# Query maxima that join the output products as exp(2m) in ten of sixteen head groups, in a fused linear-attention and MLP kernel

## The chip, the cores and the metric

The kernel runs on one core of a Trainium2 chip. Such a core has a matrix engine (TensorE, PE in the profile, with its weight loads as PEld), a vector engine (VectorE, DVE), an activation engine (ScalarE, ACT), a general engine (GpSimd, POOL) and a queue engine (SyncE, SP), which work side by side and wait for one another through semaphores. The metric is the device time of one execution in microseconds, lower is better. Matrix products land in PSUM, which has eight banks; everything else lies in SBUF.

## The reference, cut to what matters

```python
# q, k, v: (8 batches, 8 heads, 576 positions, 64); w_phi: (64, 128), all float32
def phi(x):
    proj = np.einsum('bhsd,df->bhsf', x, w_phi)
    proj = proj - np.max(np.abs(proj), axis=-1, keepdims=True)      # m, one per position
    return np.concatenate([np.exp(proj), np.exp(-proj)], axis=-1)
q_p, k_p = phi(q), phi(k)
kv  = np.einsum('bhsf,bhsd->bhfd', k_p, v)
z   = np.sum(k_p, axis=2)
num = np.einsum('bhsf,bhfd->bhsd', q_p, kv)
den = np.einsum('bhsf,bhf->bhs', q_p, z)[..., None] + 1e-06
x   = (num / den)        # -> rows of (batch, position), columns of (head, 64): 4608 x 512
h   = x @ w_in                                                       # 512 -> 2048
g   = np.where(h > 0.0, h, np.exp(np.minimum(h, 0.0)) - 1.0)         # ELU
out = g @ w_out                                                      # 2048 -> 512
```

The maximum m is taken of the absolute value and is subtracted before the sign: one half of the features is exp(p - m), the other exp(-(p - m)) = exp(-p + m). The maximum therefore does not cancel in num / den: the two halves carry the factors exp(-m) and exp(m), and their ratio is exp(2m).

## The kernel before

The 64 pairs of batch and head are worked on in 16 groups of four heads, two groups per batch. Heads lie in pairs: a 64-deep product uses one half of the rows of the array, and two products with different halves ("par" 0 and 1) stand side by side. The kernel is written as small steps, each with a letter, and a long string (`ORDER`) fixes the order in which the steps are issued; every engine works through its own instructions in that order. A digit behind a letter is the PSUM bank.

For each group, the maxima of |q w_phi| are found by a projection with positions on the partitions (`m_mm`, `m_max`). They are then needed with features on the partitions. So each maximum is split into two bf16 numbers (`m_split`), transposed on TensorE (`m_pe`), copied (`m_copy`), and subtracted from the projection by a matmul with a selector matrix of zeros and minus ones (`sel`), which accumulates on the projection:

```python
def m_split(n, part):
    ...
        mq = st["mq", n][:, :, p[0]:p[1]]
        eng = nc.gpsimd if n < PE_TRANSPOSED else nc.vector      # PE_TRANSPOSED = 4
    eng.tensor_copy(hi, mq)                                      # cast fp32 -> bf16   (L328)
    eng.tensor_tensor(mhl[n % 2][:, :, NI + p[0]:NI + p[1]], mq, hi, op=ALU.subtract)  # (L329)

def m_pe(n, part, bank=None):
    tr = transposes(bank)
    nc.tensor.transpose(tr[:, 0, :], mhl[n % 2].rearrange("p r x -> p (r x)"), ident)  # (L335)

def m_copy(n, part):
    nc.vector.tensor_copy(st["mT", n], st["trm", n][:, 0:1, :])                        # (L340)

def q_mm(n, c, bank=None):
    ...
            nc.tensor.matmul(                                    # the projection (L371)
                places(par, j, m), w_sb[rows, :], qT[rows, i:i + m, :]..., start=(x == 0), stop=False)
    for j in range(w):
        for par in range(2):
            nc.tensor.matmul(                                    # minus the maximum (L381)
                places(par, j, 1), sel[rows, p0 + j, :], mT[rows, 0, :],
                start=False, stop=(j == w - 1))

def q_exp(n, c, sg):                                             # ScalarE, both signs (L393)
    nc.scalar.activation(Eq[:, sg, ...], st["pq", n, c]..., ACT.Exp, scale=1.0 - 2.0 * sg)
```

The output products add the two halves of the features in PSUM, and VectorE divides:

```python
def x_mm(n, part, bank=None):
    for hi in range(2):
        for x, (pr, t) in enumerate(parts):
            for sg in range(2):                                  # (L439)
                nc.tensor.matmul(pn[:, hi, x, :], Eq[:, sg, hi, par, i0 * D:(i0 + 2) * D],
                                 kv_sb[:, hi, pr, sg, :], start=(sg == 0), stop=(sg == 1))

def x_div(n, part):
    nc.vector.tensor_scalar_add(den, pn[:, :, :, D], 1e-6)       # (L453)
    nc.vector.reciprocal(rec, den)                               # (L454)
    nc.vector.tensor_tensor(xp..., pn[:, :, :, 0:D], rec..., op=ALU.mult)              # (L456)
```

Other steps that the text speaks of: the k projection (`k_mm`, L238), the q projection for the maxima (`m_mm`, L294), the scaling of v by the exp of the k maxima on GpSimd (`v_scale`, L275), the products of keys and values (`kv_mm`, L409; copied out of PSUM by VectorE in L419), the DMA transposes of q and k (L227) and of the attention output (`x_dma`). The MLP works in nine chunks of 512 rows: `h_mm` (L510), exp on ScalarE (`h_exp`, L521), a clamp on GpSimd in place (`h_min`, `e_sb`, L526), a last step on VectorE (`h_elu`, L530), then `o_mm` (L538), a copy out of PSUM on ScalarE (`o_copy`, L548) and the store. The transposed attention output is held whole in SBUF (`xT_sb`, 512 x 4608); a chunk is 512 neighbouring columns of it, which belong to two batches in most chunks.

Of the kernel before, what the change touches and what calls it, by code (L numbers as in the profile page):

```python
# [10 lines left out]
FP32 = mybir.dt.float32  # L11
# [7 lines left out]
eabefegcj7dfkA0gj7BfkBeA2CA4hBl7gl6Bmj1mj0hBCM6iBkkA2DCBFEl1NDA4Bl0EmBOCFP1BEA6QBmS2CEM0CTU4eNDB  # L19
EUTOEM6VM0DP3NW4EQNM6S2NM0OTFENU6TXP1FOUQS2VP5Y4Tj1ZS6QTl0W4mTS2kTj0XTW6TkS4XA0Tj3BY2ZA6Tkl2Bp3m  # L20
Y5BCqBZrA0p4sCM2qp5rNM6qDrBNp3l2sqp7BmrsqM4rp6NFp2qsqrp5srp4CqOqrP7l3srW0sgQmp6sEj7XqS2DTrEkM0p5
NY7qTsrS0sFp4EZTsM2M6TNp5EqNS0qrp3Trp2sOsTA6fp4CqU0qrrUBssVqA2Bp5rW0sBP7p6Xqnt4qrBrsp1QCp5zqp7qr
sp0qrszW2DsrqFsS5rEp1sTXp7qp0Trfsp3qA1rtBesqp7ECoqp6qtDrBrsp5rzsqEp0sqS1qztTrrsFTsp7EU5uS1qrUrTs
A3Vt0TCtsBW1oW5BXp7A3qtCzrtsBXzt7BnM1A5M3NBtuCztDFNEM0BztNgM2uvt6ODENP7M0nM4QNES2tTNFTfS0S4TEA2t
CTp7TTU0UBA4VtBCp1qorBW2sqp0vBOXrp7quP5p4rzQsDqFW2sqrzp6XrA0qEp5szBsp3rqCvp7rqseBp4vsrqp6DsrqS0s
rM2Tp5NFEqp7sqrp3qrsTp4rsqsM0qA5rt2CEp7NBrtsBsM0qS5NtrTEsTS0U3oTA5UCTtVBt7OnBP4W0QuS3XvW5TtDXzTE
tztfFA0EuzS2M4Bt6NTztCTS4BM2otDTEtzTFA0Eut7CntNgBA4BM2CtNtBBA0OU2CUDuP6p5VQM2qM6Np4rNEp3qBsW6rqp
2sBrp5XqFeW0qsrzS6DXrp4TEzTp3sqEsvM0S6Np2TFnEqS0Tp5rqrsU6qzrUsTrp4TzOsp3qVorA0qsA6p2Brsvsp5qCP4r
p3qQCBrp4qsW0qrst2DXBEp5BFsW0zrqtEszXS6rtTvsM0A3NtBnTt5CztDBFEM0S6zNM3TtENTU0guA3S6UTotVBvt2BtTC
p1OA3qW6urp0XBP5tBQztqCzS5uA3t7DCTEntsDBFtrBEsW1TtXEA3uM5ep0NzBEp7Cqvp6rBFsM1qp5NqrM3qrS0Np2Trsf  # L30
p4qsTp7rqOsp6qrsP5rS0qQsU2oTrUsTS4Vvp7TsW0TzS2qXA4p6rBgTzp1Cqt0svqrTp7rszDW2sBEp6Xqp5rqzstrqsrA1
S3M6EsTotCFtNDt5BEtBETM6U1NFA3UBM6VtuNBvW0tCnXA6M2Bt4NBtCW0tODXuEp7vP6EA0QM2BtzNfqp6Cuzrp5BzS2qM
0Dt4rNTzFtETssvS0EU2TS6qtFoOTrtTesUTA0nVp5uCW2zqP7p6BXrvgp4BQsqzS2qA0rp7CTrzp5sqBsrp6Dsp4BEqM0qp
7NrTrsW0qsqA2rp5BXEp6BsFqp1rCqrp4sDrqsS2rp7sTEsqA5t0BrTtCFEqU1sBrUA3sS5BtVoTCtTzA1Bt7CuzW3DBEtXn
BtEDM0M2zFNW4EtXFt6nEuNM0U4vOM2NUP7tNtQVS0M2S4TNp7TOtTt3TqS0A4rop2BTtCvTtszqA0BrtCzup7sDBzp6qW4r
qvp2uXEBp3rqszA0qM4rsp7FNzrp6qECvp5sBrp4sqsp2qrDrqP7p3Qsqrp7BsrsqS5qA0srp4Brst2EqsBp3FTECp7qtrTr
sqtsrM0U4sUNA6tBVM0BS3Nt5CtODtTFEW0uP7TtEQXS2uA6t4TzCtBzW0BtXDTFtEzW0uEp7XzS2U4TzUTS0Vvt6qTrS2vT
p5Tzp4TW0qp3XqrtrqszW0rp7Xzp2qszp1rsqtsrqzsp5rsvp7sp4p3tp2uqp1vqrqt6rsqp0rsqrsqtrsqp7rsrsp5qsp4r
qsp3rqstrqsp7rstqp5rsp4qp7rqst3rqsp5rstqtrstp7t5qp4rsp2qtrqsp7rsp4qtrqsp2rstqp7rsp4qut2ruvsqp6rv
tqsutrvstt7ttp6p5qtrqsp4rst6qtrsp5tqp4rsp3qp5rqsp1rqsutrqvsut4ruvsttvtt7p6p5qtrqsup3rvstqp6rstp5  # L40
uqp4vqrp7qrsp3rsqst6rqstrsttt7utvttt6utvttt7utvttuv
# [4 lines left out]
def kernel(  # L46
# [34 lines left out]

    consts = ctx.enter_context(tc.tile_pool(name="consts", bufs=1))
# [5 lines left out]
    moep = ctx.enter_context(tc.tile_pool(name="moep", bufs=2))  # L88
    epool = ctx.enter_context(tc.tile_pool(name="epool", bufs=4))
# [24 lines left out]
    xT_sb = consts.tile([P, N_CT, NTOK], BF16)  # L114
    FULL = 4 * P

    def full_col(b):
        return (b // 2) * 2 * S + (b % 2) * (FULL + P)

    def mixed_col(b):  # L120
        return (b // 2) * 2 * S + FULL + (b % 2) * D

    def out_rows(tile_index):
        bp, t = divmod(tile_index, 9)
        rows = []
        for half in range(2):
            if t == 4:
                b, s = 2 * bp + half, 8
            else:
                b, t4 = (2 * bp, t) if t < 4 else (2 * bp + 1, t - 5)  # L130
                s = 4 * (t4 // 2) + t4 % 2 + 2 * half
            rows.append(
                out[b * S:(b + 1) * S, :].rearrange("(p s) c -> s p c", s=NS)[s]
            )
        return rows
# [11 lines left out]
    PIECES = (((0, 4), (4, 7), (7, 9)), ((0, 3), (3, 6), (6, 9)))  # L147
    TILES = (
# [56 lines left out]


# [12 lines left out]
    def t_copy(name, n, j0, j1):  # L219
        nc.vector.tensor_copy(  # L220
            get((name + "T", n), new_t(name))[:, j0:j1, :],
            st["tr", name, n, j0][:, 0:j1 - j0, :],
        )

    def t_dma(name, n):
        nat = st[name, n // 2][:, 2 * (n % 2):2 * (n % 2) + 2]
        nc.sync.dma_start_transpose(  # L227
            out=get((name + "T", n), new_t(name)),
            in_=nat.rearrange("p r s d -> p (r s d)"),
        )  # L230
# [56 lines left out]
    def m_mm(n, c, bank=None):  # L287
        own = min(n // FIRST, 1)
        p0, p1 = PIECES[own][c]
        pj = two_banks(bank).rearrange("p r (i f) -> p r i f", f=F)  # L290
        for j in range(p1 - p0):
            for par in range(2):
                rows = slice(par * D, (par + 1) * D)
                nc.tensor.matmul(  # L294
                    pj[:, par, j, :],
                    st["qT", n][rows, PLACE_OF[own][par][p0 + j], :],
                    w_sb[rows, :],
                    start=True,
                    stop=True,
                )  # L300
        st["pm", n, c] = pj

    def m_max(n, c):
        p0, p1 = PIECES[min(n // FIRST, 1)][c]
        if n < FIRST and c == 0:

            mq = st["pm", n, c][:, 0, 0, 0:2 * p1].rearrange("p (r i) -> p r i", r=2)
            st["mq0", n] = mq
        else:
            mq = get(("mq", n), lambda: small.tile([P, 2, NI], FP32, name="mq"))  # L310
            mq = mq[:, :, p0:p1]
        nc.vector.tensor_reduce(  # L312
            mq, st["pm", n, c][:, :, 0:p1 - p0, :], axis=AX.X, op=ALU.max,
            apply_absolute_value=True,
        )

    def m_split(n, part):
        if n < FIRST:
            p = ((0, 4), (4, NI))[part]
        else:  # L320
            p = (0, NI)
        hi = mhl[n % 2][:, :, p[0]:p[1]]
        if n < FIRST and part == 0:
            mq, eng = st["mq0", n], nc.vector
        else:
            mq = st["mq", n][:, :, p[0]:p[1]]
            eng = nc.gpsimd if n < PE_TRANSPOSED else nc.vector
        eng.tensor_copy(hi, mq)  # L328
        eng.tensor_tensor(  # L329
            mhl[n % 2][:, :, NI + p[0]:NI + p[1]], mq, hi, op=ALU.subtract  # L330
        )
# [6 lines left out]
    def m_copy(n, part):  # L338
        st["mT", n] = tpool.tile([P, 1, P], BF16, name="mT")
        nc.vector.tensor_copy(st["mT", n], st["trm", n][:, 0:1, :])  # L340


    def q_mm(n, c, bank=None):
# [3 lines left out]
        qT, mT = st["qT", n], st["mT", n]  # L347
# [17 lines left out]
        for x in range(max(len(r) for r in runs)):  # L365
            for par in range(2):
                if x >= len(runs[par]):
                    continue
                j, i, m = runs[par][x]
                rows = slice(par * D, (par + 1) * D)  # L370
                nc.tensor.matmul(  # L371
                    places(par, j, m),
                    w_sb[rows, :],
                    qT[rows, i:i + m, :].rearrange("p i (h t) -> p h i t", h=2),
                    start=(x == 0),
                    stop=False,
                )
        for j in range(w):
            for par in range(2):
# [4 lines left out]
                    mT[rows, 0, :],  # L384
# [32 lines left out]
    def kv_copy(n):  # L417
        st["kv", n] = work.tile([P, 2, 2, 2, D + 1], BF16, name="kv_sb")
        nc.vector.tensor_copy(  # L419
# [10 lines left out]
    def x_mm(n, part, bank=None):  # L430
        Eq, kv_sb = st["Eq", n], st["kv", n]
        parts = x_parts(n, part)
# [30 lines left out]

    def x_pe(n, part, bank=None):
# [8 lines left out]
    def x_copy(n, part):  # L473
# [3 lines left out]
        c0 = full_col(b) + part * 2 * P  # L477
        nc.vector.tensor_copy(
            xT_sb[:, 2 * g:2 * g + 2, c0:c0 + 2 * P].rearrange(
# [4 lines left out]
        if part == 1:  # L484
            nc.vector.tensor_copy(
                xT_sb[:, 2 * g:2 * g + 2, mixed_col(b):mixed_col(b) + D],
# [3 lines left out]
    def x_dma(n, pr, mixed):  # L490
        b, g = divmod(n, 2)
        xp, ct = st["xp", n, pr], 2 * g + pr
        if not mixed:
            nc.sync.dma_start_transpose(
                out=xT_sb[:, ct, full_col(b):full_col(b) + FULL].rearrange(
# [4 lines left out]
        else:  # L500
            nc.sync.dma_start_transpose(
                out=xT_sb[:, ct, mixed_col(b):mixed_col(b) + D].unsqueeze(1),
# [4 lines left out]
    def h_mm(ch, jt, h0, h1, bank=None):  # L507
        ph = psum[:, bank, h0:h1]
        for ct in range(N_CT):
# [3 lines left out]
                xT_sb[:, ct, ch * CHUNK + h0:ch * CHUNK + h1],  # L513
# [32 lines left out]
    def o_copy(ch, tt):  # L546
        st["o", ch, tt] = opool.tile([P, DM], FP32, name="o_sb")
        nc.scalar.copy(st["o", ch, tt], st["po", ch, tt])  # L548

    def o_store(ch, tt):  # L550
        last = (ch, tt) == o_tiles[-1]
        for half, rows in enumerate(out_rows(ch * (CHUNK // P) + tt)):
            queue = nc.scalar if last and half == 0 else nc.sync
            queue.dma_start(out=rows, in_=st["o", ch, tt][half * D:(half + 1) * D])

# [17 lines left out]
    def blocks(name, n):  # L573
# [3 lines left out]
    m_parts = groups((0,), first=EACH)  # L577
# [31 lines left out]
        W=(x_mm, groups(*PAIR, first=EACH)), X=(x_div, groups(*PAIR, first=EACH)),  # L609
# [9 lines left out]
    for letter, bank in re.findall(r"([A-Za-z])(\d?)", "".join(ORDER.split())):  # L619
        fn, args = queues[letter]  # L620
        fn(*next(args), **({"bank": int(bank)} if bank else {}))
    assert all(next(args, None) is None for _, args in queues.values())

# [29 lines left out]
```

## Time and profile before

The median of 3 runs is 378.05 us (377.97 to 380.45). The profiled execution spans 377.5 us with 9991 instructions; the mean granted TensorE clock is 0.991 of full speed.

| engine | busy us | share of the span |
|---|---|---|
| TensorE (PE) | 349.3 | 93% |
| weight loads (PEld) | 193.1 | 51% |
| VectorE (DVE) | 249.0 | 66% |
| ScalarE (ACT) | 248.3 | 66% |
| GpSimd (POOL) | 192.3 | 51% |

| group of instructions | count | busy us | mean ns |
|---|---|---|---|
| MLP, first product (L510) | 620 records of 640 | 137.4 | 357 |
| MLP, second product (L538) | 546 records of 576 | 133.2 | 381 |
| selector matmuls (L381) | 288 | 16.6 | 223 |
| q projection on features (L371) | 102 | 16.6 | 331 |
| output products (L439) | 640 | 25.1 | 194 |
| division, product (L456) | 32 | 26.4 | 824 |
| split of the maxima, cast (L328, on VectorE) | 12 | 6.6 | 551 |

How to read it: matmuls are pipelined, so that the duration of one is longer than the distance to the next, and the ends are modelled; what a matmul costs is better read from the starts of neighbours. Busy time of a group is the union of its records. A few per cent of the matmul records are missing. Idle time of an engine costs nothing where another one sets the pace.

### The profile page before, as it was taken

Reading aid. Unit: us, or ns where it says so; the run is one execution under the profiler, and the core shown is the slowest. Engines: PE = TensorE matmul, PEld = TensorE weight load, DVE = VectorE, ACT = ScalarE, POOL = GpSimd, SP = SyncE. Lnnn points to the kernel's source line nnn. Section 1 sums busy time; section 2 is a strip of 40 time slices with the busy share of each in tenths; the row PEclk is TensorE's granted clock in tenths of the full one; section 3 lists DMA queues with packets and bytes.
Section 4 is the critical chain, followed back from the end, with each engine's and each line's share of the span. In section 5 each row is a group of like instructions: output and inputs, shape, how many; then the busy total and the mean of one; then the engine's idle time right before and its main releaser. Section 6 shows DMA issues by size and latency. Waiting matters only on the chain.

```text
span 377.5 us, 9991 instructions
## 1 busy us (share of the span) xinstructions
PE 349.3 (93%) x4034; PEld 193.1 (51%) x4084; DVE 249.0 (66%) x441; ACT 248.3 (66%) x453; POOL 192.3 (51%) x301
## 2 busy tenths in 40 slices
PE   2777899969999999999999999999999999999995
PEld 1665676625455555544655544644555444444442
DVE  3988986794984789658868687748754473523320
ACT  3867688648887698678965898298666453514521
POOL 8851869261954396528563575518552363413310
PEclk9899999998999999999999999999999999999999
DMA  7999988799558967478984991733014300123213
GB/s 115 202 212 209 207 124 130 96 152 141 102 77 131 157 113 104 95 137 136 151 128 94 184 168 38 118 76 76 2 23 84 76 13 0 36 50 76 63 38 76
DMA packets 68158, 39.72 MB, mean 105 GB/s; under 512 B 48016, under 2 KB 62480, under 8 KB 68112
## 3 DMA queue, kind: packets, MB, share of 16 engines
q0 software_dynamic: 15856, 18.35, 31.9%
q1 hardware_dynamic: 52176, 20.59, 31.4%
q8 instruction: 32, 0.52, 0.6%
q10 hardware_dynamic: 80, 0.13, 0.1%
q14 instruction: 14, 0.11, 0.1%
HBM read 36.77 MB, written 9.44 MB: 122 GB/s over the span
## 4 chain that ended last, share of the span: by engine, by line
PE 81%; DVE 7%; POOL 5%; issue 4%; ACT 1%; DMA 1%; SPq 0%; POOLq 0%; ACTq 0%; DVEq 0%
PE banks L538 31%; PE banks L510 30%; PE banks L439 5%; PE banks L409 5%; PE banks L238 3%; PE banks L371 3%; POOL e_sb L526 2%; PE banks L294 2%; DVE mq L312 2%; PE banks L381 2%; POOL vs L275 2%; DVE mk L256 1%; DVE mhl L328 1%; DMA e_sb<-in_w_phi_dram 1%; DVE gT L530 1%
## 5 line engine op out<-in xcount | busy, mean ns | idle before, releaser
L526 POOL TENSOR_SCALAR e_sb<-e_sb 128x512 f32<-128x512 f32 (+1 forms) x160 | 90.0, 570 | 126.1 <-ACT e_sb L521 118.9
L510 PE MATMUL banks<-xT_sb,w_in_sb 128*128 128x512 bf16 (+1 forms) x620 | 137.4, 357 | 2.2 <-issue 0.6
L538 PE MATMUL banks<-w_out_sb,gT 128*128 128x512 bf16 x546 | 133.2, 381 | 3.3 <-issue 2.4
L530 DVE SCALAR_TENSOR_TENSOR gT<-e_sb,banks 128x512 bf16<-128x512 f32 (+1 forms) x160 | 96.7, 630 | 48.8 <-POOL e_sb L526 48.3
L521 ACT ACTIVATE e_sb<-banks 128x512 f32<-128x512 f32 (+1 forms) x160 | 87.2, 561 | 48.9 <-PE banks L510 41.9
L249 ACT ACTIVATE EK<-banks 128x768 bf16<-128x768 f32 x96 | 75.1, 813 | 22.2 <-PE banks L238 14.7
L393 ACT ACTIVATE Eq<-banks 128x768 bf16<-128x768 f32 (+2 forms) x96 | 73.9, 815 | 23.6 <-PE banks L381 22.9
L510 PEld LDWEIGHTS <-w_in_sb 128*128 128x128 bf16 x640 | 58.8, 98 | 59.5 <-issue 2.3
L275 POOL TENSOR_TENSOR vs<-vn,em 128x576 bf16<-128x576 bf16 x64 | 73.2, 1153 | 23.0 <-ACT em L266 22.7
L538 PEld LDWEIGHTS <-gT 128*128 128x128 bf16 x576 | 52.7, 98 | 60.4 <-issue 0.7
L256 DVE TENSOR_REDUCE mk<-banks 128x6 f32<-128x768 f32 x48 | 45.7, 954 | 15.3 <-PE banks L238 8.0
L312 DVE TENSOR_REDUCE mq<-banks 128x6 f32<-128x768 f32 (+1 forms) x46 | 42.5, 941 | 11.9 <-PE banks L294 10.2
L548 ACT COPY o_sb<-banks 128x512 f32<-128x512 f32 x36 | 21.0, 591 | 25.8 <-PE banks L538 18.9
L456 DVE TENSOR_TENSOR xp<-banks,rec 128x640 bf16<-128x640 f32 (+2 forms) x32 | 26.4, 824 | 1.1
L439 PEld LDWEIGHTS <-Eq 128*128 128x128 bf16 x640 | 23.7, 97 | 6.1 <-issue 0.9
L439 PE MATMUL banks<-kv_sb,Eq 128*128 128x65 bf16 x640 | 25.1, 194 | 0.3 <-DVE mq L312 0.2
L409 PE MATMUL banks<-vs,EK 64*128 64x65 bf16 x1152 | 23.2, 194 | 1.0 <-DVE mq L312 0.6
L409 PEld LDWEIGHTS <-EK 64*128 64x128 bf16 x1152 | 21.0, 96 | 4.1 <-issue 1.7
L238 PE MATMUL banks<-w_sb,kT 64*128 64x128 bf16 x288 | 16.6, 225 | 4.0 <-DVE kT L220 2.4
L294 PE MATMUL banks<-w_sb,qT 64*128 64x128 bf16 x288 | 16.4, 223 | 1.3 <-DVE xp L456 0.7
L371 PE MATMUL banks<-qT,w_sb 64*128 64x384 bf16 (+2 forms) x102 | 16.6, 331 | 0.9 <-DVE mq L312 0.4
L381 PE MATMUL banks<-mT,sel 64*128 64x128 bf16 x288 | 16.6, 223 | 0.0
(45 smaller groups left out, 157.2 us busy)
## 6 DMA issues: line engine op xcount, KB each, us to landing
out_dram<-o_sb SPq DMA_DIRECT2D x71, 128.0 KB, 2.5
qn<-in_q_dram POOLq DMA_DIRECT2D x7, 576.0 KB, 7.2
kn<-in_k_dram POOLq DMA_DIRECT2D x7, 576.0 KB, 7.8
vn<-in_v_dram POOLq DMA_DIRECT2D x7, 576.0 KB, 6.8
w_in_sb<-in_moe_w_in_dram POOLq DMA_DIRECT2D x2, 1024.0 KB, 20.2
w_out_sb<-in_moe_w_out_dram POOLq DMA_DIRECT2D x1, 2048.0 KB, 32.2
xT_sb<-xp SPq DMA_TRANSPOSE x56, 2.4
qn<-in_q_dram POOLq DMA_DIRECT2D x2, 288.0 KB, 6.1
```

The costliest lines, as they stand in the source:

```text
L249: nc.scalar.activation(EK[:, sg, 6 * c:6 * c + 6, :].rearrange("p (i r) f -> p r i f", r=2), st["pk", n, c], ACT.Exp, scale=1.0 - 2.0 * sg,)
L256: nc.vector.tensor_reduce(mk[:, 6 * c:6 * c + 6].rearrange("p (i r) -> p r i", r=2), st["pk", n, c], axis=AX.X, op=ALU.max, apply_absolute ...
L275: nc.gpsimd.tensor_tensor(get(("vs", n), new_vs)[:, sg, r, 0:D], st["v", n // 2][:, 2 * (n % 2) + pr], st["em", n][:, sg, r].unsqueeze(2). ...
L312: nc.vector.tensor_reduce(mq, st["pm", n, c][:, :, 0:p1 - p0, :], axis=AX.X, op=ALU.max, apply_absolute_value=True,)
L393: nc.scalar.activation(Eq[:, sg, :, :, p0 * D:p1 * D].rearrange("p h r x -> p r h x"), st["pq", n, c][:, :, 0:(p1 - p0) * P].rearrange("p ...
L409: nc.tensor.matmul(kv[:, hi, pr, sg, :], EK[rows, sg, pr * NS + s, :], vs[rows, sg, pr * NS + s, :], start=(s == 0), stop=(s == NS - 1),)
L439: nc.tensor.matmul(pn[:, hi, x, :], Eq[:, sg, hi, par, i0 * D:(i0 + 2) * D], kv_sb[:, hi, pr, sg, :], start=(sg == 0), stop=(sg == 1),)
L510: nc.tensor.matmul(ph, w_in_sb[:, ct, jt * P:(jt + 1) * P], xT_sb[:, ct, ch * CHUNK + h0:ch * CHUNK + h1], start=(ct == 0), stop=(ct == N_ ...
L521: nc.scalar.activation(e_sb, st["ph", ch, jt, h0], ACT.Exp)
L526: nc.gpsimd.tensor_scalar(e_sb, e_sb, 1.0, 0.0, op0=ALU.min, op1=ALU.max)
L530: nc.vector.scalar_tensor_tensor(gT[:, jt, h0:h1], st["e", ch, jt, h0], -1.0, st["ph", ch, jt, h0], op0=ALU.add, op1=ALU.max,)
L538: nc.tensor.matmul(po, st["gT", ch][:, jt, tt * P:(tt + 1) * P], w_out_sb[:, jt, :], start=(jt == 0), stop=(jt == N_JT - 1),)
```

## The change

In groups 6 to 15 (`JOINED = 6`) the maxima are no longer subtracted ahead of the exp. The exps of the bare projection, exp(p) and exp(-p), go into the output products, and the two halves are kept apart in PSUM. The maxima are left with positions on the partitions, where they were found, and ScalarE makes exp(m) and exp(2m) of them. VectorE then multiplies the second half by exp(2m) and adds the first; this is the reference's numerator and denominator times exp(m), so the small constant 1e-6 is multiplied by exp(m) before it is added. The split, the transpose and the selector matmuls fall away in these groups. For this the positions of q are laid out by head already in the DMA transpose, which is done in two halves.

Three further parts: the MLP's chunks are cut by batch (a chunk is the first eight positions of nine of one batch; the last chunk has the ninth of all batches), in a ring of four tiles, with one more tile for the last chunk, in place of the whole transposed output; some copies may go to the other engine (a star in `ORDER`): one q copy, five `mT` copies, three `xT` copies and seven `kv` copies to ScalarE, thirteen output copies to VectorE, the split of groups 2 and 3 to VectorE and that of 4 and 5 to GpSimd, eight of the thirty final scalings to VectorE where GpSimd does the others; and `ORDER` is new as a whole. Its purpose is to take work off TensorE and to spread copies over two engines.

```diff
+    JOINED = 6
+    M_PIECES = ((0, 4), (4, 7), (7, 10))
+    N_PIECES = ((0, 7), (7, 14), (14, 20))
+    def copy_on(scalar):
+        return nc.scalar.copy if scalar else nc.vector.tensor_copy
     def t_dma(name, n):
+        if name == "q" and n >= JOINED:
+            for hi in range(2):
+                nc.sync.dma_start_transpose(out=out_t[:, hi],
+                    in_=nat[hi * D:(hi + 1) * D].rearrange("p r s d -> p (r s d)"))
+            return
     def m_mm(n, c, bank=None):
+        if n >= JOINED:                      # 10 positions by 2 halves, 20 matmuls a group (was 18)
+            ...
+    def m_exp(n):
+        for j in range(2):                   # exp(m), exp(2m)
+            nc.scalar.activation(st["e1", n][:, j]..., st["mq", n]..., ACT.Exp, scale=1.0 + j)
-            eng = nc.gpsimd if n < PE_TRANSPOSED else nc.vector
+            eng = nc.gpsimd if (n < PE_TRANSPOSED) != other else nc.vector
     def q_mm(n, c, bank=None):
-                    stop=False,
+                    stop=n >= JOINED,
-        for j in range(w):
+        for j in range(w if n < JOINED else 0):
     def x_mm(n, part, bank=None):
+        if n >= JOINED:                      # three pieces a group (was two), halves kept apart
+            for v in range(v0, v1):
+                for sg in range(2):
+                    nc.tensor.matmul(pn[:, sg, v - v0, :], Eq[...], kv_sb[:, hi, pr, sg, :],
+                                     start=True, stop=True)
+            return
+    def x_join(n, part):
+        nc.vector.tensor_tensor(xs, pn[:, 1], st["e1", n][:, 1, v0:v1]..., op=ALU.mult)
+        nc.vector.tensor_tensor(xs, pn[:, 0], xs, op=ALU.add)
+    def x_rec(n, part):
+        nc.vector.scalar_tensor_tensor(den, st["e1", n][:, 0, v0:v1], 1e-6,
+            st["xs", n, part][:, :, D], op0=ALU.mult, op1=ALU.add)
+        nc.vector.reciprocal(st["rec", n, part], den)
+    def x_scale(n, part, other=False):
+        (nc.vector if other else nc.gpsimd).tensor_tensor(xp[:, v0:v1],
+            st["xs", n, part][:, :, 0:D], st["rec", n, part]..., op=ALU.mult)
-    xT_sb = consts.tile([P, N_CT, NTOK], BF16)
+    xT_last = consts.tile([P, N_CT, CHUNK], BF16)
+    def xT_of(ch):                           # xtp: pool of RING = 4 buffers
+        if ch == N_CHUNK - 1:
+            return xT_last
+        return get(("xT", ch), lambda: xtp.tile([P, N_CT, CHUNK], BF16, name="xT"))
-        nc.scalar.copy(st["o", ch, tt], st["po", ch, tt])
+        copy_on(not other)(st["o", ch, tt], st["po", ch, tt])
 ORDER = ...                                  # all of it new
```

(The cuts are marked by "..."; the row order of the output, `out_rows`, follows the new chunks.)

## The prediction

> **What bounds the kernel now.** I read the page from its top: busy shares, slices, then the table of stretches, because a share of the whole span hides that this kernel has a start, a middle and an end with different limits.
>
> ```profile
> PE 349.3 (93%) x4034; PEld 193.1 (51%) x4084; DVE 249.0 (66%) x441; ACT 248.3 (66%) x453; POOL 192.3 (51%) x301
> ...
> PEclk9899999998999999999999999999999999999999
> ```
>
> TensorE (PE) is busy for 349.3 of 377.5 us, so it is the bound, but not everywhere. The stretches (columns: stretch, then busy us and instruction count of PE, PEld, DVE, ACT, POOL, then granted clock):
>
> ```profile
> 0.00:60.00 60.00, 44.29 (x765) 33.97 (x766) 48.77 (x104) 41.42 (x81) 39.23 (x74) 0.97 1.02 171
> 60.00:100.00 40.00, 36.09 (x461) 20.36 (x467) 28.95 (x50) 27.50 (x53) 20.65 (x33) 0.96 0.90 127
> 100.00:280.00 180.00, 176.69 (x2253) 95.16 (x2284) 134.04 (x228) 138.78 (x250) 100.84 (x145) 1.00 0.68 108
> 280.00:377.50 97.50, 92.19 (x565) 43.61 (x571) 37.20 (x61) 40.61 (x72) 31.53 (x51) 1.00 0.23 50
> ```
>
> The reader is to see where PE is idle: 15.7 us in the first 60, 3.9 in the next 40, only 3.3 in the 180 after that, 5.3 at the end (nearly all of it after the last matmul). From 100 us on, only less TensorE work makes the kernel shorter; in the first 100 us other engines can. The chain of waits agrees: up to 23 us it lies mostly on VectorE (DVE), from 34 to 65 us mostly on GpSimd (POOL: the e_sb clamps and the scaling of v).
>
> The one large hole between 60 and 100 us is this (timeline: start us, us, engine, line):
>
> ```profile
> 78.60 3.23 DVE L328 CAST mhl<-mq 128x18 bf16<-128x18 f32 x1
> 78.70 2.27 POOL L275 TENSOR_TENSOR vs<-vn,em 128x576 bf16<-128x576 bf16 x2
> ...
> 82.10 0.23 PE L335 MATMUL banks<-ident,mhl 128*128 128x128 bf16 x1 [2.62 <-DVE mhl L329]
> ```
>
> A cast of 18 elements, which takes 0.17 us in most of its other records, took 3.23 us while POOL ran; TensorE waited 2.62 us for what follows it, and its clock in the 20 us from 80 on is 0.91, which is another 0.09 x 20 = 1.8 us. This hole cost about 4 us.
>
> **What the Trainium skill says.** "SBUF — State Buffer", section Who interferes with whom: VectorE and GpSimd share one port pair, held as an exclusive lock for a whole instruction; a VectorE copy or cast from SBUF to SBUF takes it, and so does a VectorE instruction with two SBUF inputs against a GpSimd one that reads SBUF. The trace agrees for the cast (3.23, 0.82, 0.62 and 0.55 us, each beside a POOL instruction, 0.17 to 0.18 otherwise); for two SBUF inputs it has only L329, always 0.18 us and never begun behind a running POOL instruction, so it shows nothing. "TensorE: Matmul & The Clock Gate", section What's actually happening: an idle window of about 3.4 us halves the clock; the 0.91 after the hole agrees. "VectorE: DVE Perf Modes", section Why PSUM operands drop a tier: fp32 work out of PSUM runs one element per cycle; the trace has L456 at 692, 824 and 957 ns for 512, 640 and 768 elements, 1.035 ns each plus 162 ns.
>
> **The change part by part.** Joined groups are 6 to 15, ten of sixteen.
>
> TensorE. 288 selector matmuls become 108: 180 fewer. Their price must be read with care:
>
> ```profile
> 151.92 0.34 PE L371 MATMUL banks<-qT,w_sb 64*128 64x384 bf16 x2
> 152.09 0.33 PE L381 MATMUL banks<-mT,sel 64*128 64x128 bf16 x6
> 152.35 0.82 PE L538 MATMUL banks<-w_out_sb,gT 128*128 128x512 bf16 x3
> ```
>
> The durations overlap, so I take start to start. Six selectors here take 152.35 - 152.09 = 0.26 us, and that would give 180 x 0.043 = 7.8 us. But 0.09 of it is the step from 64-row matmuls to a full-height one, which stays, after L371 instead. Six 64-row matmuls followed by other 64-row ones take 0.18 us (L238 at 200.03, L294 at 200.21), and the chain counts the selectors 0.17 us per six. So I choose 0.028 us each: 180 x 0.028 = 5.1 us off. Ten transposes of the split maxima (L335) go: 10 x 0.07 = 0.7 us off. The q maxima need 20 matmuls a group in place of 18: 10 x 2 x 0.028 = 0.6 us on. The output products stay at 40 a group, without accumulation; nothing there. Sum: **5.2 us less on TensorE**, all of it on the bound.
>
> VectorE. Off, in the joined groups: ten cast and subtract pairs (0.551 + 0.181 us, means of L328 and L329), 7.3; ten mT copies (0.218), 2.2; twenty divisions (0.165 + 0.216 + 0.824), 24.1; seven kv copies that go to ScalarE (0.696), 4.9: 38.5 us. On: per group three pairs of products of 455, 455 and 390 elements out of PSUM; by the 1.035 ns and 162 ns above 0.633, 0.633 and 0.566 each, 60 of them, 36.6; thirty small multiply-adds and reciprocals (0.18 + 0.21), 11.7; maxima 256 elements longer a group, 10 x 0.27 = 2.7; eight final scalings, about 0.58 each, 4.6; thirteen output copies taken from ScalarE, 0.69 each by the kv copy's 696 ns for 520 elements, 9.0: 64.6 us. Net about 26 us on, less 0.08 us per added instruction, as neighbours overlap (two L530 in a row start 0.60 us apart and take 0.68): **some 23 us more on VectorE between 90 and 290 us**. Off the early part: five mT copies, one qT and three xT copies go to ScalarE and two split pairs to POOL, two pairs come back: about 4 us less. In the middle stretch VectorE goes from 134 us to about 134 + 23 x 180/200 = 155 us in perhaps 176, from 74% to 88%.
>
> ScalarE: 20 small exps (0.211) and 7 kv copies (about 0.6) on, 13 output copies (0.591) off, the early copies some 3 us on: +4 us, no new bound. POOL: 22 final scalings, at L275's 1153/576 = 2.0 ns per element 0.90 or 0.77 us, 19 us on: 51% to 57%. DMA: the q transposes of joined groups come in two halves, 10 more issues on the SyncE queue, 1.4 us each, where the transfers' share is 0.68 in the middle: hidden. The MLP's dependence on batches hardly moves: a chunk needs its own batch alone and the last one all of them, while before the last two chunks needed the last batches too. The ring of 4 keeps a batch from writing until the chunk four back has been read; TensorE's order puts that reading well ahead.
>
> On the path, then: TensorE 5.2 us less. The hole at 78.6 us: its cast goes to POOL for groups 4 and 5 and vanishes after, about 4 us; I count 3, as groups 2 and 3 get the cast on VectorE. The start, where VectorE has 4 us less: I count 1.5, as POOL bounds its second half and is not relieved. Against that, waits in the middle, where VectorE is at 88% and work in order must wait for it: I count 3. Sum: 5.2 + 3 + 1.5 - 3 = 6.7 us less, 378.05 - 6.7 = **371.3**; I say 371.
>
> **The rivals.** First, VectorE takes the bound over in the middle. For it: 88%, and thirty multiply-adds with two SBUF inputs, each of which may stand behind a POOL instruction (0.6 to 1.15 us) if the skill is right; at 57% POOL and some 0.5 us each that is up to 30 x 0.57 x 0.5 = 8 us of VectorE, which lifts it to 92%. Against it: the order of the middle was made anew, and the present one keeps PE at 98% with ScalarE at 77%. It would make the time 374 to 379. Second, the start gains more: with copies on two engines the whole 19.6 us of PE idle time before 100 us shrinks by 5 or 6, and the middle stays at 98%; for it, that the moved copies are those of the first groups, on the chain up to 23 us; against it, the POOL stretch from 34 to 65 us. It would make 364 to 368. Third, the selectors cost 0.043 us after all, with the step to full height gone into them: 2.7 us more gain, 368 to 369. Fourth, half-height q transposes land late: the queue's landings are 4.2 us now and two q tiles are in flight; I give it little, and 375 if it holds.
>
> **Range and chances.** The known term, 5.2 us, is 1.4%, under the 2% line at 370.5; faster by over 2% needs the start or the hole to give 2.4 us more than the middle takes. My sum is just short of the line, with an uncertainty of some 4 us. So 365 to 377 for 8 in 10; faster 0.43, same 0.53, slower 0.04, since slower means 7.6 us lost where TensorE has less to do.
>
> **What would show it.** Selector row at x108 and some 6 us busy; PE busy near 344; middle stretch with 3 to 6 us PE idle where 3.3 stood, and DVE about 88%; no VectorE cast of over 1 us holding PE between 60 and 100 us. If DVE waits for POOL at the small multiply-adds (durations spread from 0.18 to over 1 us), the first rival is at work; if PE is idle under 15 us before 100 us, the second. I am wrong most easily in the 3 us that I give the middle and the 4.5 us that I give the first 100 us: both are judgement, not sums.

## The result, and the profile after

The changed kernel takes 367.62 us (median of 4 runs, 366.58 to 371.29); beside it the kernel before took 378.9. The ratio is 0.9705, with a 95% interval of 0.9633 to 0.9777: about 11 us less, where the prediction said 371 and 7 us less. The time lies in the predicted range; faster by over 2%, to which the prediction gave 0.43 against 0.53 for the same, is what happened.

The profiled execution is the slowest one of the changed kernel (371.29 us, span 369.5). First the busy shares of its page, with the clock by slices:

```profile
PE 344.7 (93%) x3865; PEld 189.8 (51%) x3914; DVE 269.1 (73%) x475; ACT 251.0 (68%) x477; POOL 212.7 (58%) x323
...
PEclk9999999999999989999999999999999999999999
```

The same stretches as in the prediction (the last is shorter, as the span is), columns as there:

```profile
0.00:60.00 60.00, 48.03 (x789) 36.32 (x792) 48.56 (x101) 45.56 (x94) 39.61 (x71) 1.00 1.01 168
60.00:100.00 40.00, 39.31 (x501) 21.88 (x505) 32.28 (x55) 32.62 (x63) 27.38 (x47) 1.00 0.78 130
100.00:280.00 180.00, 172.83 (x2163) 92.59 (x2194) 148.01 (x253) 139.85 (x265) 115.48 (x159) 0.99 0.71 110
280.00:369.50 89.50, 84.49 (x419) 39.00 (x426) 40.24 (x69) 33.00 (x57) 30.23 (x48) 0.99 0.24 51
```

The reader is to see three things. PE is idle 12.0 us in the first 60 (15.7 before) and 0.7 in the next 40 (3.9 before), and its clock there is 1.00 in both (0.97 and 0.96 before). VectorE carries 20 us more over the span, 14 of them in the middle stretch. And the middle seems to have got worse, with 7.2 us of PE idle time for 3.3. That last reading needs care, for two reasons. 3.4 us of it is one hole, which the waits of PE in this stretch name:

```profile
PE banks L267 <- DMA kT<-kn: 3.4, 1, 3.4
PE banks L661 <- issue: 2.1, 13, 0.2
PE banks L510 <- DVE kv_sb L487: 0.5, 1, 0.5
```

A slice at a lower clock followed it (0.91 over the 20 us from 120 on). Behind the hole stands a DMA transpose of k that took 14.52 us to land, where the median of its kind in this trace is 4.9. The chain of waits has it (start, length, what):

```profile
114.56 7.93 DMA kn<-in_k_dram
122.49 0.02 issue
122.51 14.52 DMA kT<-kn
```

The hole and the clock behind it fit the profiled execution being some 4 us over the median; four others of this kernel had spans of 364.5 to 366.2 us and a clock of 0.998 or more. The second reason is the record itself: 30 of the 576 second-product matmuls and 18 of the 576 first-product ones that read the ring have no record here; before, it was 30 of 576 and 20 of 640. Each missing one leaves a gap that counts as idle. Some of the experiments below left complete records, and their middle stretches are the fair comparison. First the kernel before with nine copies moved (experiment 6), then the changed kernel with zero selectors put back (experiment 1), then the changed kernel with its early placements undone (experiment 2), each in its own answer:

```profile
100.00:280.00 180.00, 179.85 (x2284) 95.10 (x2282) 134.12 (x228) 138.85 (x250) 101.00 (x145) 1.00 0.67 108
```

```profile
100.00:280.00 180.00, 179.35 (x2374) 96.71 (x2374) 148.15 (x253) 140.63 (x266) 115.78 (x159) 1.00 0.71 110
```

```profile
100.00:280.00 180.00, 179.18 (x2229) 93.46 (x2228) 153.23 (x259) 144.25 (x274) 120.18 (x166) 1.00 0.73 114
```

PE is idle 0.15 us in the first, 0.65 in the second and 0.82 in the third. The third counts most, since the second gives TensorE extra work that may cover waits. The 3.3 us that the prediction started from was almost wholly missing records, and the middle became worse by 0.5 to 0.7 us, the late transpose aside.

### The profile page after: what moved, and what is told of

The parts are those of the page before. It is cut to its first block, busy times and chain, and to the rows that moved or that the text cites. A ratio compares the mean times of both kernels' runs of the same rounds, so it can differ in the third digit from the quotient of the medians.

```text
span 369.5 us, 9757 instructions
## 1 busy us (share of the span) xinstructions
PE 344.7 (93%) x3865; PEld 189.8 (51%) x3914; DVE 269.1 (73%) x475; ACT 251.0 (68%) x477; POOL 212.7 (58%) x323
## 4 chain that ended last, share of the span: by engine, by line
PE 76%; DVE 11%; DMA 8%; issue 2%; POOL 1%; ACT 1%; DVEq 0%; ACTq 0%; POOLq 0%
PE banks L661 31%; PE banks L633 29%; PE banks L477 4%; DMA kT<-kn 4%; PE banks L510 3%; DVE mk L285 3%; PE banks L267 2%; PE banks L437 2%; DMA kn<-in_k_dram 2%; DMA qn<-in_q_dram 2%; DVE gT L653 2%; DVE mq L368 2%; PE banks L526 2%; PE banks L326 1%; DVE xp L543 1%
## 5 line engine op out<-in xcount | busy, mean ns | idle before, releaser
L633 PE MATMUL banks<-xT,w_in_sb 128*128 128x512 bf16 (+1 forms) x558 | 122.0, 355 | 2.0 <-DVE gT L653 0.3
L354 DVE TENSOR_REDUCE mx<-banks 128x6 f32<-128x768 f32 (+1 forms) x30 | 30.7, 1038 | 4.9 <-PE banks L326 3.8
L576 POOL TENSOR_TENSOR xj<-xs,recj 128x448 bf16<-128x448 f32 (+1 forms) x22 | 20.0, 914 | 17.4 <-DVE recj L571 9.8
L477 PEld LDWEIGHTS <-EK 64*128 64x128 bf16 x1152 | 22.1, 99 | 2.9 <-issue 1.3
L555 DVE TENSOR_TENSOR xs<-banks,e 128x455 f32<-128x455 f32 (+1 forms) x30 | 18.0, 602 | 7.2 <-PE banks L510 5.8
L671 ACT COPY o_sb<-banks 128x512 f32<-128x512 f32 x23 | 13.4, 591 | 14.5 <-PE banks L661 14.5
L510 PEld LDWEIGHTS <-Eq 128*128 128x128 bf16 x400 | 16.1, 97 | 7.3 <-issue 1.3
L560 DVE TENSOR_TENSOR xs<-banks,xs 128x455 f32<-128x455 f32 (+1 forms) x30 | 18.3, 609 | 1.1
L267 PEld LDWEIGHTS <-kT 64*128 64x128 bf16 x288 | 10.0, 99 | 15.5 <-issue 9.1
L510 PE MATMUL banks<-kv_sb,Eq 128*128 128x65 bf16 x400 | 17.3, 194 | 0.5 <-DVE kv_sb L487 0.5
```

Source lines behind the costliest of these rows:

```text
L267: nc.tensor.matmul(pj[:, par, i3, :], st["kT", n][rows, 3 * c + i3, :], w_sb[rows, :], start=True, stop=True,)
L477: nc.tensor.matmul(kv[:, hi, pr, sg, :], EK[rows, sg, pr * NS + s, :], vs[rows, sg, pr * NS + s, :], start=(s == 0), stop=(s == NS - 1),)
L510: nc.tensor.matmul(pn[:, sg, v - v0, :], Eq[:, sg, hi, par, i0 * D:(i0 + 2) * D], kv_sb[:, hi, pr, sg, :], start=True, stop=True,)
L633: nc.tensor.matmul(ph, w_in_sb[:, ct, jt * P:(jt + 1) * P], xT_of(ch)[:, ct, h0:h1], start=(ct == 0), stop=(ct == N_CT - 1),)
```

## The experiments

Each kernel was timed beside the kernel before on one chip, so differences are worked out from the ratios: the difference of two ratios times 379 us, which is where the kernel before stood in all of them. The changed kernel is 0.9705, with an interval of 2.7 us to either side, mostly from its one execution with the late transpose. Every difference against it is therefore uncertain by some 3 us, and where it matters the difference of the medians stands beside it; the expectations used these medians (6.6 and 10.4 us, where the ratios give 5.7 and 10.0). Three of the ten executions in experiment 2 and one of the four in experiment 4 were slow ones, over 1.5% above the fastest of their kernel, and the ratios leave them out.

**1. What the selectors cost.** The 180 selector matmuls back, accumulating a tile of zeros:

```diff
-                    stop=n >= JOINED,
+                    stop=False,
-        for j in range(w if n < JOINED else 0):
+        for j in range(w):
-                    st["mT", n][rows, 0, :],
+                    (st["mT", n][rows, 0, :] if n < JOINED else zeros[rows, :]),
```

> The changed kernel, with the 180 selector matmuls of the joined groups put back on TensorE, accumulating zeros, so that the result does not change. If a selector costs 0.028 us (the prediction's reading): 5.1 us more, about 372.7. If it costs 0.043 us: 7.8 us more, about 375.4. If TensorE is no longer the bound in the middle stretch, under 2 us more.

Measured: 372.34 us, ratio 0.9818 (0.9793 to 0.9844); 0.0113 x 379 = 4.3 us more, or 4.7 by the medians. That is 0.024 to 0.026 us a selector, close to the 0.028 that the prediction chose; with the 3 us of uncertainty it is at most 7.2 us, still under the 7.8 that 0.043 would give. The traces settle the price without the total. This run has, with the zero selectors between the projection and a full-height matmul:

```profile
191.20 0.32 PE L439 MATMUL banks<-qT,w_sb 64*128 64x384 bf16 x2
191.36 0.33 PE L451 MATMUL banks<-zeros,sel 64*128 64x128 bf16 x6
191.62 1.04 PE L663 MATMUL banks<-w_out_sb,gT 128*128 128x512 bf16 x4
```

The changed kernel has the projection directly ahead of a full-height one:

```profile
178.79 0.33 PE L437 MATMUL banks<-qT,w_sb 64*128 64x384 bf16 x2
179.05 1.25 PE L633 MATMUL banks<-xT,w_in_sb 128*128 128x512 bf16 x5
```

The step to full height (0.26 us after the first of the small ones) is there in both, so six selectors add only the 0.16 us from 191.20 to 191.36, or 0.17 as the mean of such places: 0.028 each, 5.0 us for 180. So TensorE's own work comes out in the time nearly in full.

**2. The early placements, both kinds.** The stars of the q, mT and xT copies and of the splits ignored, the order as the change has it:

```diff
-        if star:
+        if star and letter not in "mQZO":
             how["other"] = True
```

> The changed kernel with the early copies back on VectorE (one q copy, five mT, three xT) and the splits back where they were (groups 2 and 3 on GpSimd, 4 and 5 on VectorE), the order of steps unchanged. If the placement of this early work made the gain of the first 100 us: 3 to 6 us more, 371 to 374, with PE idle again 15 us or more before 60 us, or a hole of 2 us or more behind a cast at group 4 or 5. If the new order made it, within 1.5 us of 367.6.

Measured: 374.25 us, ratio 0.9856 (0.9828 to 0.9885): 5.7 us more. In its profile PE is idle 14.6 us before 60 us and 3.1 us from 60 to 100. The hole is back as well: a cast of maxima took 2.74 us at 76.06. By the medians it is 6.6 us more. So where this early work runs is worth at least as much as the removed selectors.

**3. Only the copies.** As above with `"mQZ"`.

> The changed kernel with only the nine early copies back on VectorE, the splits left as the change has them. Undoing copies and splits together cost 6.6 us. If the copies, which lie on the chain of the first 25 us, carry it: 3 to 4 us more, 371, with PE idle 2.5 us more before 60 us. If the splits carry nearly all of it: within 1 us of 367.6.

Measured: 368.54 us, ratio 0.9747, with an interval of 0.968 to 0.9814: one of its four runs had the late k transpose again (3.3 us of PE idle). By the medians 0.9 us more. The copies alone carry little; the wide interval allows no finer word.

**4. Only the splits.** As above with `"O"`.

> The changed kernel with only the splits back where they were (groups 2 and 3 on GpSimd, 4 and 5 on VectorE). If a VectorE cast of group 4 or 5 is again caught beside GpSimd: 2 to 4 us more, about 371, and TensorE waits 2 us for it between 60 and 100 us. If the new order keeps the cast clear of GpSimd: within 1 us of 367.6.

Measured: 371.61 us, ratio 0.9793 (0.9761 to 0.9825): 3.3 us more, or 4.0 by the medians. Its timeline shows the hole again (VectorE, then GpSimd, then PE):

```profile
73.00 2.74 DVE L394 CAST mhl<-mq 128x18 bf16<-128x18 f32 x1
```

```profile
73.43 2.27 POOL L304 TENSOR_TENSOR vs<-vn,em 128x576 bf16<-128x576 bf16 x2
```

```profile
76.01 0.23 PE L401 MATMUL banks<-ident,mhl 128*128 128x128 bf16 x1 [1.97 <-DVE mhl L395]
```

The cast ends 0.04 us after the two GpSimd products do (73.00 + 2.74 against 73.43 + 2.27). PE waits 1.97 us, and the clock from 60 to 100 us drops to 0.96.

**5. The same split, in the kernel before.** All splits on GpSimd:

```diff
-            eng = nc.gpsimd if n < PE_TRANSPOSED else nc.vector
+            eng = nc.gpsimd
```

> The kernel before with the splits of all groups on GpSimd, nothing else changed. If the cast of group 4 that waited 3.23 us beside GpSimd is what cost the hole at 79 us: about 4 us less, 374, and no hole there. If TensorE would wait there anyway for the maxima: 1 us less or nothing.

Measured: 376.21 us, ratio 0.9927 (0.9903 to 0.995): 2.8 us less. At the place of the old hole its timeline has:

```profile
78.67 0.21 POOL L328 CAST mhl<-mq 128x18 bf16<-128x18 f32 x1
78.97 0.22 POOL L329 TENSOR_TENSOR mhl<-mq,mhl 128x18 bf16<-128x18 f32 x1
79.16 2.25 POOL L275 TENSOR_TENSOR vs<-vn,em 128x576 bf16<-128x576 bf16 x2
...
79.31 0.22 PE L335 MATMUL banks<-ident,mhl 128*128 128x128 bf16 x1
```

The transpose that began at 82.10 begins at 79.31. The edit moves the splits of twelve groups, but the gain lies here: PE is idle 1.05 us from 60 to 100 where it was 3.9, and the clock there is 1.00 for 0.96. The hole came from the engine of an 18-element cast, and goes away with it without anything else of the change.

**6. The copies, in the kernel before.** The same nine copies on ScalarE:

```diff
-        nc.vector.tensor_copy(st["mT", n], st["trm", n][:, 0:1, :])
+        (nc.scalar.copy if (n, part) in ((1, 0), (0, 1), (1, 1), (3, 0), (5, 0))
+         else nc.vector.tensor_copy)(st["mT", n], st["trm", n][:, 0:1, :])
         # likewise the copy ("q", 1, 5) and the xT copies of (0, 0), (1, 0), (0, 1)
```

> The kernel before with only the early copies on ScalarE (the q copy, five mT copies, three xT copies), in its own order. If the engine of these copies is what shortened the start: 2 to 4 us less, 374 to 376. If it takes the new order: within 1 us of 378.

Measured: 379.26 us, ratio 1.0011 (0.9995 to 1.0027): nothing. PE idle before 60 us goes from 15.7 to 15.2. The moved copies do not shorten this start, whose order was made without them.

**7. Both, in the kernel before.** Experiment 6, with splits of groups 2 and 3 on VectorE and of 4 and later on GpSimd.

> The kernel before with all the early placements of the change (nine copies on ScalarE, splits of groups 2 and 3 on VectorE and of 4 and later on GpSimd), in its own order. The splits of groups 4 and later on GpSimd gave 2.9 us there, the copies nothing. If placement alone makes the early gain: 5 us or more less, 374 or below. If the order was made for it and is needed: about 376, as with the splits alone.

Measured: 376.17 us, ratio 0.9927 (0.9899 to 0.9955): 2.8 us less, as with the splits alone. In the changed kernel the same placements are worth 5.7. The difference, some 3 us, is no larger than its uncertainty, but the traces point the same way: the placements take PE's idle time before 60 us from 15.7 to 15.0 here, and from 14.6 to 12.0 in the changed kernel. So a part of the gain belongs to order and placement together. The new order was not run in the kernel before, so that it is not separated here from the other parts of the change.

**8. The late placements.** Output copies all on ScalarE, kv copies all on VectorE, final scalings all on GpSimd (`"uVy"` ignored).

> The changed kernel with the late copies back (output copies all on ScalarE, kv copies all on VectorE) and all thirty final scalings on GpSimd. VectorE has some 8 us less then, ScalarE 4 us more, GpSimd 7 us more. If the middle of the change has slack on all three, as its near lack of PE idle time says: within 1 us of 367.6. If the copies on two engines were needed there: 2 us or more above.

Measured: 368.41 us, ratio 0.9714 (0.9681 to 0.9747): 0.3 us more (0.8 by the medians), within what is measured. The spreading of late copies, which took thirteen output copies onto VectorE, is not where the time came from.

**9. More VectorE work in the middle.** Thirty further copies out of PSUM, one behind each join:

```diff
         nc.vector.tensor_tensor(xs, pn[:, 0], xs, op=ALU.add)
         st["xs", n, part] = xs
+        nc.vector.tensor_copy(spare[...], pn[:, 0]...)        # read by nothing
```

> The changed kernel with thirty further VectorE copies out of PSUM, one behind each join, which nothing reads (about 0.6 us each, 17 us in all): VectorE goes from some 82 to some 91% of the middle stretch. If VectorE still has slack there: under 1.5 us more. If it is at its limit, as the prediction's first rival has it: 5 to 15 us more, with PE waiting for VectorE in the middle.

Measured: 379.66 us, ratio 1.0018 (1.0001 to 1.0036): 11.9 us more for 18.0 us of copies, the whole gain gone. Of PE's waits between 100 and 300 us, 5.9 us were for the copies themselves (L563), which hold the PSUM banks; hence the next two.

**10. The same without the banks.** A maximum over a constant SBUF tile in place of the copy:

```diff
+        nc.vector.tensor_reduce(spare, sel.rearrange("p i f -> p (i f)")[:, 0:(v1 - v0) * (D + 1)],
+                                axis=AX.X, op=ALU.max)        # read by nothing
```

> The changed kernel with thirty further VectorE maxima over an SBUF tile that is constant, one behind each join, which nothing reads: as long as the copies of the run before (about 0.55 us each, 17 us in all), but no PSUM bank is held longer by them. The copies cost 12 us. If it was VectorE's time that cost: 10 to 12 us more than 367.6 again. If it was the banks that were held: under 4 us more.

Measured: 377.98 us, ratio 0.9968 (0.9953 to 0.9984): 10.0 us more for 17.8 us. PE's waits between 100 and 300 us, the longest that are not issue time:

```profile
PE banks L438 <- DVE gT L655: 2.1, 2, 1.9
...
PE banks L663 <- DVE gT L655: 1.9, 4, 0.6
PE banks L635 <- DVE gT L655: 1.3, 3, 0.6
```

PE now waits for the MLP's last VectorE step, which stands behind the added work in VectorE's order. So the cost stays when the copies no longer hold the banks: it is VectorE's time.

**11. Half of it.** The same in even groups only.

> The changed kernel with fifteen of the thirty maxima over the constant SBUF tile (those of the even groups), some 8.5 us of VectorE. The thirty cost 10.4 us for 17. If every microsecond of VectorE costs the same there, 5 us more, about 372.8. If there is a slack of some 6.5 us that is used up first, 2 us more, about 369.6.

Measured: 372.98 us, ratio 0.9826 (0.9788 to 0.9865): 4.6 us more (5.4 by the medians) for 8.9 us. In its profiled execution, the slowest of the four, PE also waited 2.3 us for a transpose of k. A slack of 6.5 us that is used up first is unlikely, though the interval does not rule out a smaller one; by these runs each microsecond of VectorE put behind a join costs some 0.5 to 0.7. So in the middle it is not TensorE alone that sets the pace. Taking VectorE work out elsewhere (experiment 8) gained nothing, though ScalarE and GpSimd took it over there. Whether VectorE's load or the place in the join's chain is what costs was not told apart.

**12. No cast of maxima on VectorE.** The changed kernel with the splits of groups 2 and 3 on GpSimd as well.

> The changed kernel with the splits of groups 2 and 3 on GpSimd too, so that no cast of maxima from SBUF is left on VectorE. If GpSimd bounds that part of the start: 0 to 2 us more. If a cast there still waits for GpSimd: 0.5 to 1 us less, about 367, a version that beats both.

Measured: 367.54 us, ratio 0.9697 (0.966 to 0.9734): the same as the change, so this is no version that beats it.

## Why the prediction was right, point by point

**TensorE, 5.2 us less: right.** The selectors measured 4.3 to 4.7 for the predicted 5.1, and 5.0 by the starts in the trace (experiment 1), and their row in the groups of the changed kernel is as foreseen:

```profile
L449 PE MATMUL banks<-mT,sel 64*128 64x128 bf16 x108 | 6.3, 223 | 0.0
```

The choice of 0.028 over 0.043 was the right one, and the third rival falls. The transposes and the longer maxima were not measured by themselves.

**The hole at 79 us, 3 us less: right.** 2.8 us in the kernel before, 3.3 in the changed one (experiments 5 and 4).

**The start, 1.5 us less: too little.** PE is idle 3.7 us less before 60 us, and the granted clock from 0 to 20 us is 1.00 where it was 0.91. All early placements together are worth 5.7 us in the new order, the hole's 3.3 included. The term failed in how it was judged: it weighed VectorE's 4 us against GpSimd's bound, as if the order stayed. Experiments 2 and 7 suggest that the placements pay more in the order made for them. With the hole, PE's idle time before 100 us went from 19.6 to 12.7 us, under the 15 us that the prediction named as the sign of the second rival, while the middle stayed full. So the second rival is what came: 6.9 us for its 5 or 6, and a time inside its 364 to 368.

**The middle, 3 us more: wrong.** It cost 0.5 to 0.7 us (0.65 and 0.82 of PE idle against 0.15 in complete records). The first rival, VectorE as the bound, did not come. The expected load was mis-sized: VectorE got 20 us more in all, as summed (23 less 4), but 14 of it in the middle instead of 21, so that its share there is 82% and not 88%; from 60 to 100 us it has 3.3 more and after 280 us 3.0 more. The waits behind GpSimd were mis-sized too. The changed kernel's groups have:

```profile
L567 DVE SCALAR_TENSOR_TENSOR denj<-e,xs 128x7 f32<-128x7 f32 (+1 forms) x30 | 6.0, 199 | 0.2
L576 DVE TENSOR_TENSOR xj<-xs,recj 128x384 bf16<-128x384 f32 (+1 forms) x8 | 6.0, 744 | 0.1
```

The multiply-adds took 199 ns on average, not 180 plus some 280; only four of thirty were above 0.21 us (0.37 to 0.53). The final scalings on VectorE, also with two SBUF inputs, took 744 for 580, as two of the eight were long (0.95 and 1.55 us). But the rival was near: 8.9 us more of VectorE behind the joins cost 4.6 (experiment 11), and 17.8 to 18.0 us cost 10.0 to 11.9 (experiments 9 and 10).

**The fourth rival, late transposes:** the half transposes of q held PE nowhere in the middle; the slowest landed after 6.5 us, where 6.9 was the slowest before. Whole transposes of k did, which the prediction did not name. The slowest of k took 10.3 to 17.0 us in the ten profiles of the changed kernel and its variants, and 8.7 to 9.3 in the four of the kernel before and its variants; in four of the ten PE waited for one, 0.7 to 3.4 us. So the change brought late transposes, of another tile than the rival said. Whether the added halves on the same queue make them, or the new order, is open.

**The sum.** The change is 11.2 us by the ratio: 4.3 for the selectors and 5.7 for the early placements in their order, which leaves 1.2 to the rest, less than the uncertainty of either. The prediction's 6.7 was short by the start's term and by a loss in the middle that did not happen. Both were named as judgement, and both erred to the same side; the miss of 4.5 us is a little more than the 4 us that the prediction gave its sum, and only the wider range covers it.

## What to carry to other kernels

Price a small matmul from the start of one to the start of the next of its kind, with the switch to another shape left out; that gave the cost of 180 of them within a fifth here. Ahead of reading idle time of TensorE in a full stretch, compare the number of records with the number of instructions. And look for tiny VectorE instructions with a long duration beside GpSimd: moving the splits of the maxima, one cast of which was caught, was worth some 3 us here, as much as two thirds of the 180 removed matmuls.

## What the runs showed of the hardware that was not expected

The Trainium skill, "SBUF — State Buffer", section Who interferes with whom, says that a VectorE instruction with two SBUF inputs and a GpSimd one that reads SBUF block each other. The trace before could not show it; the trace after does. A final scaling of 384 elements, 0.55 us in four of its six records, took 1.55 us at 228.95, when GpSimd had begun at 228.94 (VectorE, then GpSimd):

```profile
228.95 1.55 DVE L576 TENSOR_TENSOR xj<-xs,recj 128x384 bf16<-128x384 f32 x1
```

```profile
228.94 2.57 POOL L304 TENSOR_TENSOR vs<-vn,em 128x576 bf16<-128x576 bf16 x2 [1.42 <-ACT em L295]
```

It ended before the second GpSimd product did, and the pair took 2.57 us where two take 2.27 elsewhere: this fits a wait for one GpSimd instruction and not for the run of them, while the cast at 73.00 in experiment 4 waited for both.

The casts caught longest also began while GpSimd was issuing a DMA, ahead of the products that the prediction and experiment 4 show. In experiment 4:

```profile
72.57 0.83 POOL L201 DMA_DIRECT2D qn<-in_q_dram  x1
```

In the kernel before a second issue follows the products:

```profile
77.84 0.83 POOL L192 DMA_DIRECT2D vn<-in_v_dram  x1
...
81.04 0.80 POOL L192 DMA_DIRECT2D qn<-in_q_dram  x1
```

There the cast ended at 81.83, 0.86 us after the products (78.70 + 2.27) and 0.01 before the end of that second issue. So "beside GpSimd" includes its DMA issues; which of these instructions held the cast was not tried.
